# Turning the normalised tokens of two tiles by DMA instead of TensorE, with the instruction order and buffer slots of an adaLN attention and MLP block laid out again

## The chip, the cores and the metric

One core of a Trainium2 chip runs the whole program. The metric is the device time in microseconds of one launch, as the median of several executions. A profile of one execution stands beside it; its span runs from the first to the last instruction.

## The reference

The input is one sequence of 2048 tokens of width 448, in bf16. A conditioning row gives six modulation vectors. The first half of the block normalises the tokens, scales and shifts them, and runs attention with 16 heads of width 28 in which each token looks at itself and at seven earlier tokens, two apart. The second half normalises again, scales, shifts, normalises a third time inside the MLP branch, and applies a two-layer MLP of width 1792.

```python
mod = (silu(c) @ w_mod).reshape(1, 6, 1, 448)
sa, ca, ga, sb, cb, gb = mod[:, 0..5]
h = layernorm(x) * (1 + ca) + sa
x = x + ga * A(h)          # A: qkv, window of 8 with dilation 2, softmax, @ wo
h = layernorm(x) * (1 + cb) + sb
x = x + gb * B(h)          # B: layernorm, gelu(@ w1 + b1), @ w2 + b2
```

## The kernel before

Even and odd tokens are held as two streams (`NS = 2`), so that a dilation of 2 becomes a plain window. There are eight tiles of 2 x 128 tokens and nine attention batches of 2 x 114 queries. Tiles are taken in units: tile 0, tile 1, tiles 2 and 3, tiles 4 and 5, tiles 6 and 7.

For each unit the function `front_ln` issues on VectorE (DVE) the statistics (line 450), their aggregation (452) and the normalisation (470) into a token tile `zy`; the inverse root is made on ScalarE (459 and 461) for tiles 0 and 1, and on GpSimd (466) for the others. A small copy of the last columns, `tail` (480 to 484), completes `zy`. The tokens then have to be turned so that the features stand on the partitions. There are two ways to do it:

- by TensorE: eight transposes for each tile (line 527) into PSUM tiles `ptr`;
- by DMA: one transposing DMA for each tile on SyncE's queue (line 519) into an SBUF tile `zT`.

Either way `affine` (494 on DVE, 496 on ScalarE) scales and shifts the four 128-row pieces into `hT`, from which TensorE makes queries, keys (lines 540, 546, 562) and values (700). For tiles 2 to 7 the queries and keys come out in token order and are turned by DMA too (624).

The other names used below: `c_cols` (line 385) and `mod_cols` (406) are the small matmuls that make the first modulation columns; `sca` (421) adds them up on DVE. `mods` (634) makes the other four modulation rows, `mod_rows` (639) copies them out, and two DMAs (641 and 643) bring them to all partitions as `mod_bc`. `mod_bc` scales the output projection weights on DVE (646), which `out_proj` (797) needs. Then follow the residual (804) and the second and third normalisation, which end in the transposing DMA `yT` (828), and the MLP: first layer at lines 540 and 546, gelu at 858, second layer at 877, final sum at 883, store at 887. `filler` (378) issues products of a tile of zeros; they only keep TensorE occupied.

No scheduler runs on the chip. The code first builds a list of 699 numbered tasks, each with the engines it may run on. The string `ORDER` then lists the numbers in the order of issue. `:A`, `:D`, `:P` put a task on ScalarE, DVE or GpSimd instead of its usual engine, `:R` takes the 64-row part of a sum first, and `55+8@55` puts eight zero products into the PSUM tile of task 55 ahead of it. `SLOTS` gives the memory slot of each buffer in the order in which the buffers are made; a buffer waits until the last reader of its slot is done. Every engine works through its own tasks in that order, SyncE's DMA queue included.

These are the task numbers that matter here:

| tasks | what |
|---|---|
| 17 to 41 | loads on SyncE's queue: 27 is x of tiles 2 and 3, 33 to 36 the four `wmod` pieces for `mods`, 37 to 40 `wo` |
| 55; 63, 64; 68, 69 | `c_cols`; `mod_cols` of the 128-row part; `mod_cols` of the 64-row part |
| 80, 116 | transposes of tiles 0 and 1 by TensorE |
| 95 to 99, 101 to 105 | queries and keys of tile 0 |
| 121 to 126 | queries and keys of tile 1 and their copies |
| 138, 148 | the turn of tile 2 and of tile 3 |
| 149 to 152 | the four `affine` pieces of tiles 2 and 3 |
| 153, 156 | keys and queries of tile 2 |
| 165, 167, 168 | `mods`, its store, `mod_bc` |
| 179, 228 | values of batches 0 and 1 |
| 181, 184; 230, 233 | logits of batch 0; of batch 1 |
| 187, 188 | denominators and outputs of batch 0 |
| 201, 211 | the DMA turn of tiles 4 and 5 |

Of the kernel before, what the change touches and what calls it, by code (L numbers as in the profile page):

```python
# [14 lines left out]
S, D, H, DH, F = 2048, 448, 16, 28, 1792  # L15
# [19 lines left out]
UNITS = [[0], [1], [2, 3], [4, 5], [6, 7]]  # L35
# [5 lines left out]
ENGINE = {"A": "ACT", "D": "DVE", "P": "POOL", "R": "PE2"}  # L41
RATE = 310e3
SLOTS = [
# [6 lines left out]
]  # L50
# [7 lines left out]
232 278 39 40 41 299:R 235 280 211 267 279 268 270 269 300 236 238 281 239 155 158 159 237 304 301 305 271 160:D 302 162  # L58
201 167 215 163 214 212 213 240 225:R 188 226 303 306 282 168 169 170 307 309 191 308 310 311 219:R 220 272 284 241 283
242 245 164 161 312 42 171 313 339 286 285:A 336 221 246 337 340 314 243 216:R 43 44 244 217 290 247 45 46 218 550:A 291  # L60
292 316 317 315 341 318 287:R 288 222 223 248 250 249 338 319 441:P 251 252 320 321 342 127 255 344 322 128 345 334:R
335 369 370 374 323 324 253 254 256 326 257 371 551:R 224 47 48 49 327 325 328 375 372 376 373 552 296 297 343 377 329
331 379 330 332:D 258 260 259 261:A 346 378 380 381 442:R 347 348 50 174 173 351 349 51 289 333 262 382 52 53 443 586:A
352 175 350 353 477:A 405 404 409 408 354 383 355 386 356 387 406 423 426 420:R 421 407 422 410 413 414 411 412 176 357
384 385 388 172 177 358 415:R 418 419 416 436 434 359 361 362 389 391 360 390 392 54 178 363 227 393 396 394 417 364 397
483 395 440 398 484 447 435 448 366 365 444 445 480 481 399 478:R 479 367 400 427 401 402 485 449 446 437 482 486 488
450 452 293 438 294 487 451 453 454 489 490 298 368 403 513 514:R 516 515 518 517 532 535 424 491 492 455 456 457 493
458 495 459 524 526 527 496 494 497 460 461 536 425 498 528 500 499 525 462 463 501 295 502 505 503 504 464 465 466 467
469 519:R 520 521 529 531 522 523 430 431 530 468 470 549 592 553 556 554 557 506 471 558 555 593 594 507 428 472 508
429 432 587 588 474 589 559 560 433 543 544 590 561 591 473 475:A 509 510 511 562 596 595 563 545 546 597 598 476 599  # L70
564 565 566 600 567 568 601 512 623 547 602 548 622 626 627 638:R 639 640 624 625 569 570 628 630 629 633:R 637 632 634
534 636 604 605 603 606 571 573 572 607 609 574 608 610 611 539 575 578 579 614 615 576 612 577 580 540 631 635 537 652
538 653 654 655 581 613 616 617 583 618 619 582 584:A 641 620:A 621 585 644 658 659 661 662 660 533 645 656 541 542 657
663:R 439 667 664 665 666 676 680 677 679 648 646 668 670 669 673:R 674 672 647 649 695 678 675 671 681 683 682 684 696
642 643 650 685 686 651 697 687 688 689 690 698 691 692 693 694
"""


# [73 lines left out]
def kernel(  # L152
# [18 lines left out]
    P = Plan()  # L171
# [302 lines left out]
    def xn(p, n):  # L474
        return x_all[:, p, n * D:(n + 1) * D]
# [26 lines left out]
    def front_ln(u, on_act, dma=False):  # L502
        np_ = len(u)
        if dma:
            zT = sb("yT", [128, NS * KT, 256], BF16, "zT")
        else:
            ptr = [psum("ptr", (128, np_, 2, NS, 128), BF16) for _ in range(2)]
        for q, p in enumerate(u):
            z = fixed("zy", zys)
            for n in range(NS):  # L510
                stats(lambda p=p, n=n: xn(p, n), 0, 2 * p + n, [f"x{p}"])
            rstd(0, 2 * p, 2, on_act)
            for n in range(NS):
                normalize(lambda z=z, n=n: z.t[:, n, 0:D], lambda p=p, n=n: xn(p, n), 0, 2 * p + n, [f"x{p}"],
                          bufs=[z], writes=[(z, n)])
            tail(z, [(z, 0), (z, 1)], (z, 2), p == 0)
            zk = [(z, 0), (z, 1), (z, 2)]
            if dma:
                add("SP", 2.0, lambda z=z, q=q: nc.sync.dma_start_transpose(
                    out=zT.t[:, :, 128 * q:128 * q + 128], in_=z.t[:].rearrange("p n e -> p (n e)")), reads=zk, bufs=[z, zT],  # L520
                    writes=[(zT, q)], xfer=1.0, name=f"zT{p}")
                continue

            def tr(q=q, z=z):
                for kt in range(KT):
                    for n in range(NS):
                        nc.tensor.transpose(out=ptr[kt % 2].t[:, q, kt // 2, n, :], in_=z.t[:, n, kt * 128:(kt + 1) * 128], identity=ident[:])
# [373 lines left out]
    for pi, (batches, tiles) in enumerate(PHASES):  # L901
        exps.clear()
        lt_mms.clear()
        for i in batches:
            if i < 3:
                front_ln(UNITS[i + 2], False, dma=i > 0)
                if UNITS[i + 2][0] in NATURAL:
                    for p in UNITS[i + 2]:
                        natural_qk(p)
                else:  # L910
                    front_qk(UNITS[i + 2])
            if i == 0:
                mods()
            attention(i, tbl, prev_w1)
            while done < NP and (128 * (done + 1) - 1) // SBQ <= i:
                out_proj(done)
                done += 1
        tg = add("ACT", 1.28, lambda: nc.scalar.preload_act_table_set(GELU_SET), after=list(exps), name="tbl")
        gelus.clear()
        w1_mms.clear()  # L920
        for t in tiles:
            mlp(t, tg, list(lt_mms))
        prev_w1 = list(w1_mms)
        if pi < len(PHASES) - 1:
            tbl = add("ACT", 1.28, lambda: nc.scalar.preload_act_table_set(EXP_SET), after=list(gelus), name="tbl")
# [30 lines left out]
```

## Time and profile before

| what | us |
|---|---|
| median of 3 executions | 173.84 (173.5 to 174.85) |
| the profiled execution | 173.98 |
| its span | 171.9 |
| TensorE busy | 163.9 |
| DVE busy | 116.0 |
| ScalarE busy | 107.6 |
| GpSimd busy | 46.2 |

The profiled execution is 2.1 us longer than its span and 0.14 us above the median. In the lists of the trace each row starts with the start and the length in us, then engine, line and operation, output and inputs, shape and count; in square brackets stands how long the engine had been idle, and who ended that. "PE" is TensorE's multiplication, "PEld" its weight load; a name ending in q is an engine's sequencer, so that "SPq" is SyncE issuing DMAs. A matmul's length is longer than its share of the engine, because matmuls overlap: twelve that start one after the other 0.19 us apart are each shown as 0.35 us long. What one costs is the distance between starts.

### The profile page before, as it was taken

The page shows a single profiled execution, that of the slowest core. Times are in us where ns is not written, and L with a number is a line of the kernel's source. Part 1 is how long each engine was busy: PE and PEld are TensorE (multiplying, and loading weights), DVE is VectorE, ACT ScalarE, POOL GpSimd, SP SyncE. Part 2 cuts the span into 40 slices and gives each one's busy share as a digit, 9 for nine tenths or more (in the row PEclk, how much of TensorE's full clock was granted, in tenths as well). Part 3 has the DMA queues.
Part 4 walks back from the last instruction along what each step waited for, and adds up shares of the span by engine and source line. Part 5 has one row for each costly group of instructions (what it writes and reads, how often), then busy time and mean ns, then how long its engine had stood idle before and what let it go on. Part 6 is the DMA issues. An engine that isn't in the chain of part 4 may idle for free.

```text
span 171.9 us, 5019 instructions
## 1 busy us (share of the span) xinstructions
PE 163.9 (95%) x2142; PEld 84.5 (49%) x2142; DVE 116.0 (67%) x282; ACT 107.6 (63%) x149; POOL 46.2 (27%) x76
## 2 busy tenths in 40 slices
PE   5699998999999999999999999999999999999992
PEld 3476654455545543345454345555334543445562
DVE  5648989698999989998644895756997704001032
ACT  3437999989489993789896569664285402817000
POOL 3270611600260401525005701130113701930000
PEclk9999999999999999999999999999999999999999
DMA  5999908799999999102540000151100063100013
GB/s 160 342 300 400 206 6 96 153 197 160 232 240 210 227 165 251 21 0 53 75 65 6 0 0 4 57 106 20 53 0 0 0 122 125 39 0 0 0 57 107
DMA packets 33462, 18.27 MB, mean 106 GB/s; under 512 B 26395, under 2 KB 32480, under 8 KB 33440
## 3 DMA queue, kind: packets, MB, share of 16 engines
q1 hardware_dynamic: 33436, 17.95, 45.8%
q8 instruction: 17, 0.28, 0.7%
q14 instruction: 5, 0.04, 0.1%
q10 hardware_dynamic: 4, 0.00, 0.0%
HBM read 9.81 MB, written 1.84 MB: 68 GB/s over the span
## 4 chain that ended last, share of the span: by engine, by line
PE 61%; DVE 21%; DMA 6%; ACT 4%; POOL 3%; issue 2%; SPq 0%; POOLq 0%; DVEq 0%
PE p L877 23%; PE p L540 22%; DVE stt L450 8%; PE pw L797 5%; PE p L546 4%; DVE zy L470 3%; DMA yT<-zy 2%; POOL rs_all L466 2%; PE ps_col L378 2%; DMA mod_bc<-mod_hbm 2%; DVE mvs L452 2%; DVE h L813 2%; DVE et L745 2%; DMA x_all<-in_A_x_dram 2%; ACT hm L858 1%
## 5 line engine op out<-in xcount | busy, mean ns | idle before, releaser
L858 ACT ACTIVATE hm<-p,b_col 128x512 bf16<-128x512 f32 x56 | 33.9, 689 | 30.7 <-PE p L546 26.2
L877 PE MATMUL p<-w_s,hm 128*128 128x448 bf16 (+1 forms) x238 | 44.1, 342 | 0.0
L540 PE MATMUL p<-yT,w_s 128*128 128x512 bf16 x168 | 38.5, 380 | 0.6 <-DMA yT<-zy 0.6
L466 POOL TENSOR_TENSOR rs_all<-tv_all,neg_half 128x2 f32<-128x2 f32 x22 | 16.7, 764 | 59.3 <-DVE tv_all L464 51.8
L877 PEld LDWEIGHTS <-hm 128*128 128x128 bf16 x238 | 22.8, 98 | 19.2 <-issue 0.4
L883 DVE TENSOR_TENSOR x_all<-p,x1p 128x896 bf16<-128x896 f32 (+2 forms) x10 | 8.8, 900 | 27.6 <-PE p L877 27.6
L540 PEld LDWEIGHTS <-w_s 128*128 128x128 bf16 x168 | 15.6, 98 | 22.2 <-issue 4.4
L450 DVE BATCH_NORM_STATS2 stt<-x_all 128x6 f32<-128x448 bf16 x32 | 19.0, 611 | 0.6 <-DMA x_all<-in_A_x_dram 0.5
L739 ACT ACTIVATE et<-lt 128x928 bf16<-128x928 f32 x18 | 16.1, 948 | 2.4 <-PE lt L732 2.3
L835 POOL TENSOR_TENSOR x1p<-x_all,gbb_bc 128x448 f32<-128x448 bf16 x16 | 16.3, 1047 | 0.2 <-issue 0.2
L540 PE MATMUL pq<-wqk_st,hT 128*128 128x448 bf16 x72 | 15.2, 354 | 0.0
L782 DVE TENSOR_TENSOR qT<-po,den 128x912 bf16<-128x912 f32 x9 | 9.8, 1104 | 6.0 <-ACT den L776 6.0
L745 DVE TENSOR_TENSOR et<-et,mask 128x928 bf16<-128x928 bf16 x18 | 11.1, 641 | 3.4 <-ACT et L739 3.2
L797 PE MATMUL pw<-wo_s,qT 128*128 128x448 bf16 x64 | 12.8, 353 | 0.1
L621 ACT CAST zy<-pq 128x896 bf16<-128x896 f32 x11 | 10.0, 910 | 1.7 <-PE pq L546 0.9
L804 DVE TENSOR_TENSOR x_all<-pw,x_all 128x896 bf16<-128x896 f32 x8 | 8.7, 1086 | 3.4 <-PE pw L797 3.3
L813 DVE TENSOR_TENSOR h<-h,mod_bc 128x896 bf16<-128x896 bf16 x16 | 10.6, 665 | 0.2
L540 PEld LDWEIGHTS <-hT 128*128 128x128 bf16 x72 | 6.4, 98 | 7.0 <-issue 1.8
L776 ACT ACTIVATE den<-den,den_bias 128x928 f32<-128x928 f32 x9 | 9.5, 1066 | 0.2
L774 ACT ACTIVATE den<-pd 128x928 f32<-128x928 f32 x9 | 8.4, 948 | 1.8 <-DVE qT L782 1.2
L450 DVE BATCH_NORM_STATS2 stt<-h 128x6 f32<-128x448 bf16 x16 | 9.3, 613 | 0.2
L470 DVE TENSOR_SCALAR zy<-h,mvs,rs_all 128x448 bf16<-128x448 bf16 x16 | 8.6, 579 | 1.1 <-POOL rs_all L466 1.0
(113 smaller groups left out, 190.9 us busy)
## 6 DMA issues: line engine op xcount, KB each, us to landing
w_s<-in_B_w_dram SPq DMA_DIRECT2D x7, 224.0 KB
out_dram<-x_all SPq DMA_DIRECT2D x7, 224.0 KB, 2.1
x_all<-in_A_x_dram SPq DMA_DIRECT2D x3, 448.0 KB, 6.2
wmod<-in_w_mod_dram SPq DMA_DIRECT2D x3, 448.0 KB, 8.7
w_s<-in_B_w_dram SPq DMA_DIRECT2D x3, 448.0 KB
wqk_st<-in_A_wqkv_dram SPq DMA_DIRECT2D x3, 225.0 KB
wm_st<-in_w_mod_dram SPq DMA_DIRECT2D x1, 672.0 KB, 4.6
x_all<-in_A_x_dram SPq DMA_DIRECT2D x2, 224.0 KB
```

The source lines that it names most:

```text
L450: add("DVE", 0.53, lambda: nc.vector.bn_stats(out=stt[:, w, b, :], in_=src()), reads=reads, bufs=bufs, after=early if w == b == 0 else (), ...
L466: add("POOL", 0.55 + 0.17 * n, lambda: nc.gpsimd.tensor_tensor(out=r, in0=tv, in1=neg_half[:, 0:n], op=ALU.pow), reads=[f"tv{w}_{b0}", "ne ...
L470: add("DVE", 0.31, lambda: nc.vector.tensor_scalar(out=dst(), in0=src(), scalar1=mvs[:, w, b, 0:1], scalar2=rs_all[:, w, b:b + 1], op0=ALU ...
L540: nc.tensor.matmul(out(), lhsT=lhs(kt, slice(0, 128)), rhs=rhs(kt, slice(0, 128)), start=first and kt == 0, stop=not first and kt == KT - 2)
L621: add("ACT", 0.80, lambda to=to, src=src: nc.scalar.copy(out=to(), in_=src()), bufs=[pq, st], reads=["zpad"], writes=[(st, 0)], name="evac ...
L739: exps.append(add("ACT", 0.83, lambda half=half, lt=lt: nc.scalar.activation(out=et.t[:, 2 * half:2 * half + 2].rearrange("p r m c -> p r ...
L745: nc.vector.tensor_tensor(out=ev, in0=ev, in1=mask[:], op=ALU.mult)
L797: nc.tensor.matmul(pw.t[:, s, 0:D], lhsT=qT[:, KT * s + ft, LEAD + 128 * p:LEAD + 128 * p + 128], rhs=wo_s[:, ft, :], start=(ft == 0), sto ...
L813: add("DVE", 0.55, lambda vec=vec, op=op: nc.vector.tensor_tensor(out=h2.t[:], in0=h2.t[:], in1=vec.unsqueeze(1).to_broadcast([128, NS, D] ...
L835: add("POOL", 1.0, lambda n=n: nc.gpsimd.tensor_tensor(out=x1p.t[:, n, :], in0=xn(p, n), in1=gbb2_bc[:], op=ALU.add), reads=[f"x{p}", "gbb ...
L858: gelus.append(add("ACT", 0.585, lambda f=f, a=a, p1=p1s[g]: nc.scalar.activation(out=hm.t[:, f].rearrange("p n c -> p (n c)"), in_=p1.t[: ...
L877: nc.tensor.matmul(p2.t[:, n, 0:c1 - c0], lhsT=hm.t[:, f, n, q * 128:(q + 1) * 128], rhs=w2_s[:, f, c0:c1], start=(f == parts[0][0]), stop ...
```

## The change

`front_ln` is now called with `dma=True` for the unit of tiles 2 and 3 as well. Its two PSUM tiles `ptr` give way to one SBUF tile `zT`, so there is one buffer less. Tasks 138 and 148 move from TensorE to SyncE's queue, and the numbers of all other tasks stay. `SLOTS` and `ORDER` are written anew as a whole; their beginnings are shown here.

```diff
 SLOTS = [
-    0, 1, 1, 1, 0, 0, 1, 1, 2, 0, 3, 0, 1, 2, 0, 3, 1, 0, 2, 1, 3, 1, 2, 3, ...
+    1, 0, 1, 0, 0, 1, 3, 1, 0, 2, 3, 0, 1, 0, 2, 3, 2, 2, 3, 0, 1, 3, 2, 1, ...
 ORDER = """
-17 18 0 15 14 1 55+8@55 9 12 5 3 10 2 13 19 20 21 22 91:P 23 24 25 26 92:P 87:P 93:P 94:P 88:P 89:P 7 27 28 16 56 73 74
-11 6 71 57 58 72 75 59 60 76 78 77 67 61 79 63+14@63 66 62 85:A 90:A 68+3@68 69 64 4 65 70 80 81 29 30 83 95+5@95 101 82
-102 103 109 107 108 110 86:A 111 31 96 97 84 104 32 33 34 35 105 112 98 114 113 115:A 106 116 139 120:A 118:A 117:A
-119:A 131 36 37 99 100 132 129 130 133 134 179 180 121 122:R 123 141 140 142 143 144 136 135 137 146 145 273 204 205 38
-138 8 147 148 151 152:A 150:A 202 203 206 124 125:R 126 184 185 181 182 149 156:R 157 153 207 208 192 193 209 210:D 275
-183 194 186 195 154 196 276 274 277 197 230 233 231 165 166 187 234 228+5@228 189 190 229 265 266 263 264 199 198 200
+17 15 14 16 0 1 2 9 13 6 11 12 18 5 73 74 71 72 3 10 19 20 21 22 86:P 91:P 23 24 55+11@55 56 57 58 59 75 60 85:P 76 77
+68+12@68 67 66 69 78 79 63+4@63 61 62 64 4 65 25 70 26 89:P 90:A 27 80 92:A 83 81 101+13@101 93:A 82 107 102 103 109
+95+2@95 108 110 84 111 112 113 114 28 94:P 104 105:R 115:A 116 106 96 87:P 7 120:A 97 118:A 29 141 30 31 32 88:P 98 99:R
+33 139 142 129 100 140 143 144 131 179 184 181 130 132 133 134 145 146 147:D 148 135 136 192 137 119:A 117:A 121:R 122
+182 124:R 125 138 194 8 193 204 195 196 185 186 183 197 187 123 180 188 199 198 126:D 230 149:A 189 200 233 231 234 151
+150 152 153+3@153 154 34 35 156:R 157 263 264 275 205 202 203 206 265 207 209 232 235 208 201 190 191 266 267 210:D 273
 ...
-                front_ln(UNITS[i + 2], False, dma=i > 0)
+                front_ln(UNITS[i + 2], False, dma=True)
```

The zero products of the order before are 8 at task 55, 14 at 63, 3 at 68, 5 at 95 and 5 at 228, 35 in all. In the order after they are 11 at task 55, 12 at 68, 4 at 63, 13 at 101, 2 at 95, 3 at 153 and 5 at 228, 50 in all. The seventh to ninth entries of `SLOTS` are the PSUM slots of `c_cols` and of the two `mod_cols`: 1, 1, 2 before and 3, 1, 0 after. On SyncE's queue the order after is: load 33, turn of tile 3, turn of tile 2, loads 34 and 35, turn of tile 4, loads 36 and 37, then the turned keys and queries of tile 2, the turn of tile 5, the store of `mods`, loads 38 to 40, and `mod_bc`. Before, loads 33 to 41 were issued first, then the turns.

More of the change, by code (lines that the diff above doesn't have):

```diff
@@ L61 @@
[L61 to L75, printed above, removed]
+17 15 14 16 0 1 2 9 13 6 11 12 18 5 73 74 71 72 3 10 19 20 21 22 86:P 91:P 23 24 55+11@55 56 57 58 59 75 60 85:P 76 77
@@ new lines @@
+228+5@228 229 36 165 37 268 155 158 269 274 276 270 277 211 166 236 299:R 238 167 278 280 239 279 281 212 271 214 215
+159:R 301 300 160 304 237 240 38 213:A 39 162:R 302 303 225 305 40 163 306 307 168 169 170 272 308 309 310 311 226 282
+219:R 220 286 241 441:A 285:A 242 243 245 312 313 161 164 216 336 339 284:A 316 283:A 550:P 290:R 337 314 315 317 318
+244 41 221 42 43 44 45 227 340 341 217 319 218 321 287 46 291 288 320 322 338 222:R 223 246 247 248 323 326 342 250 127
+128 249 324 251 252 344 345 253 255 327 256 325 328 329 369:R 370 289 47 334 335 371 372 373 374 254 257 375 296 297 376
@@ new lines @@
+551:R 552 224 48 378 49 377 258 330 331 332:D 259 379 260 333 343 346 380 381 261 262 50 442:R 443 347 348 382 349 351
+352 383 386 384 405 404 408 420:R 409 421 422 410 406 407 415:R 51 171 477:P 350 353 385 387 388 52 53 177 176 54 292
+389 354 391 390 173 355 356 175 413 412 414 411 172 436 392 393 419 357 416 417 418 394 395 396 178 397 398 399 423 434
+174 358 400 427 359 360 361 362 363 364 426 401 402:D 403 440 480 444 481 445 483 435 293 447 484 294 478:R 446 365 366
+367:A 485 482 486 437 448 488 449 450 479:D 487 451 438 452 489 453 454 368 514:R 513 515 516 518 517 455 532 536 534
@@ new lines @@
+535 490 491 524 528 526 586:A 525 527 492 456 459 457 519:R 520 523 533 529:R 460 521 495 425 493 496 458 461 424 462
+430 431 463 464 494 465 295 298 592 531 530 522 549 593 556 553 554 497 498 428 429 587 499 500 466 469 501 557 502 470
+505 506 467 468 471 503 555 558 560 559 432 588 589 504 594 472 474 473 590 507 508 509 475:D 510 561 511:D 591 543 544
+596 595 545 546 562 563 564 439 433 597 598 599 565 568 566 600 601 547 569 567 570 604 602 512 476 623 622 624 625
+638:R 639 626 640 641 627 571 573 572 605 603 606 607 608 609 574 628 631 630 632 633:R 629 610 611 575 578 576 577 612
@@ L76 @@
+614 637 579 615 580 613 616 581 582 654 537 538 539 617 583 619 618 620 584 635 585 644 621 652 634 636 645 653 655 540
+658 660 662 659 661 548 656 541 676 678 642 663:R 667 664 666 648 665 657 542 649 668 672 671 677 673:R 681 670 669 674
+675 683 684 695 682 646 647 696 687 685 643 680 697 679 698 686 650 651 688 689 690 691 692 693 694
 """
```

3 lines of the change are left out of this document (removed), and 12 rows, old and new, of the table SLOTS.

## The prediction

> **What bounds the kernel now.** The first views read are the busy lines of the page with its table of slices, then the busy time by stage, then the chain of work that ended last.
>
> ```profile
> PE 163.9 (95%) x2142; PEld 84.5 (49%) x2142; DVE 116.0 (67%) x282; ACT 107.6 (63%) x149; POOL 46.2 (27%) x76
> ...
> PEclk9999999999999999999999999999999999999999
> DMA  5999908799999999102540000151100063100013
> ```
>
> ```profile
> 11.87:41.42 29.55, 28.74 (x614) 16.51 (x613) 25.82 (x68) 26.19 (x36) 8.04 (x15) 1.00 0.87 185
> 41.42:64.72 23.30, 22.67 (x394) 11.62 (x395) 22.21 (x50) 20.27 (x24) 6.01 (x6) 1.00 0.99 206
> 64.72:169.00 104.28, 103.97 (x1062) 50.48 (x1062) 61.68 (x129) 57.30 (x83) 26.77 (x35) 1.00 0.20 45
> ```
>
> ```profile
> 5.81 3.15 PE ps_col L378 x14
> ...
> 10.58 0.76 PE ptr L527 x8
> ...
> 13.78 0.70 DVE zy L470 x2
> 14.48 1.07 DVE stt L450 x2
> ...
> 60.55 4.03 DMA yT<-zy
> 64.58 0.14 issue
> 64.72 2.75 PE p L540 x12
> ```
>
> In a stage row the first number behind the stage is its length, the next is TensorE's busy time, then come its weight loads, DVE, ScalarE and GpSimd. From 64.72 us, where the MLP begins, TensorE is busy 103.97 of 104.28 us. From 11.87, where the first sums start, to 41.42 it is busy 28.74 of 29.55, and to 64.72 another 22.67 of 23.30. So TensorE bounds everything from 11.87 on. The chain names DVE and a DMA ahead of 64.72, but TensorE waits there for 0.6 us only: both would have to come sooner to bring a gain. A change pays by starting TensorE sooner, by taking work from it, or by taking away one of its few waits, and costs what new waits it brings.
>
> **The start.** These are the rows of TensorE and of who waits for it.
>
> ```profile
> 1.26 1.89 PE L378 MATMUL ps_c<-warm_w 128*128 128x256 bf16 x8 [1.26 <-DVE warm_w L242]
> ...
> 3.42 0.60 PE L385 MATMUL ps_c<-one,c_row 1*128 1x128 bf16 x4 [0.28 <-DMA c_row<-in_c_dram]
> ...
> 5.81 3.15 PE L378 MATMUL ps_col<-warm_w 128*128 128x256 bf16 x14 [1.79 <-DVE silu_bf L392]
> ...
> 10.62 0.17 DVE L421 TENSOR_TENSOR mod_col<-ps_col,add_col 128x8 f32<-128x8 f32 x1 [2.98 <-PE ps_col L406]
> ...
> 11.16 0.71 PE L378 MATMUL pq<-warm_w 128*128 128x256 bf16 x5
> 11.25 1.02 ACT L496 ACTIVATE hT<-ptr,mod_col 128x256 bf16<-128x256 bf16 x2 [3.36 <-PE ptr L527]
> ...
> 11.87 1.58 PE L562 MATMUL pq<-hT,Wqk 128*128 128x256 bf16 x12
> ```
>
> The fourteen zero products at 5.81 waited 1.79 us for `silu_bf`, because their PSUM tile has the slot of `c_cols` (both 1), which `silu` reads. DVE then stood still for 2.98 us and ScalarE for 3.36. Starts lie about 0.21 us apart in the first two groups (3.15 less a last length of 0.4, over 13) and about 0.11 in the third (0.71 less 0.27, over 4).
>
> In the new slots the three tiles have slots 3, 1 and 0, so the twelve products of task 68 need not wait for `silu`. Eleven products from 1.26 end at 1.26 + 11 x 0.21 = 3.6, `c_cols` at 4.2, and twelve more at 6.7. The `mod_cols` take about 1 us (from 8.96, where the row of 5.81 ends, to 10.58, less 0.6 for three zero products between), and four products 0.4 to 0.8. The transposes of tile 0 then run from about 8.4 to 9.1 instead of 10.58 to 11.34: some 2 us sooner for DVE and ScalarE. But thirteen zero products now stand ahead of the first sums instead of five. At 0.11 they take 1.4 us, and the first sums start at about 10.5 to 10.8, as ScalarE, which makes its second piece of `hT` 1.02 us after the transposes, also allows. I take 10.8, a gain of 1.1. One bound is 10.3, a gain of 1.6. The other is thirteen at 0.21, which is 2.7 us: 11.8 to 12.1, a loss of up to 0.2.
>
> **The turns of tiles 2 and 3.** These rows bear on what is taken from TensorE and on what the DMA costs.
>
> ```profile
> 19.51 1.08 PE L527 MATMUL ptr<-ident,zy 128*128 128x128 bf16 x16
> 20.43 0.82 PE L540 MATMUL pq<-hT,Wqk 128*128 128x256 bf16 x6
> ...
> 22.27 0.70 PE L732 MATMUL lt<-qT,kT 28*64 28x58 bf16 x64
> 23.06 0.37 PE L546 MATMUL pq<-wqr_st,hT 64*128 64x448 bf16 x2
> ...
> 27.37 0.54 PE L754 MATMUL pd<-et,ones_k 64*32 64x464 bf16 x8
> ...
> 32.49 0.87 PEld L540 LDWEIGHTS <-hT 128*128 128x128 bf16 x6 [0.21 <-issue]
> ...
> 34.03 0.68 PE L765 MATMUL po<-et,vb 64*32 64x57 bf16 x64
> ```
>
> ```profile
> L335 SPq DMA_DIRECT2D x_all<-in_A_x_dram x5: 397/468/586, 0.8 to 9.4; - x5
> ...
> DMA to landing us min/median/max: 6.2/6.2/6.2
> ```
>
> ```profile
> L358 SPq DMA_DIRECT2D wmod<-in_w_mod_dram x4: 328/480/665, 10.0 to 13.7; - x4
> ...
> DMA to landing us min/median/max: 8.5/8.6/8.9
> ```
>
> ```profile
> L494 DVE TENSOR_SCALAR hT<-zT,mod_col x7: 403/406/501, 35.1 to 45.8; 128x512 bf16<-128x512 bf16 x7
> L519 SPq DMA_TRANSPOSE zT<-zy x4: 1232/1286/2126, 25.1 to 35.4; - x4
> ...
> DMA to landing us min/median/max: 3.2/3.2/3.2
> ```
>
> Taken away: from 19.51 to the next start at 20.43 the sixteen transposes hold TensorE for 0.92 us. That is the second term.
>
> Added: two issues of 1.3 us on SyncE, 3.2 us each from issue to landing. When are they issued? The x of tiles 2 and 3 is asked for at 6.4 and lands 6.2 us later, at 12.6. DVE then has four statistics (two in 1.07), two normalisations (0.70 both) and about 1 us of small pieces, some 4 us in all: tile 3 is ready near 16.6, and the second turn is issued at 17.9. The last load ahead of them, the first `wmod` piece, is asked for at 10.0 and lands at 18.6 by its row. Undisturbed the two land at 19.8 and 21.1. Were they as slow as the loads, 8.6 us each, they would land at 25.2 and 26.5. I take 21.5, nearer the first, because the other three `wmod` pieces are now issued behind them, and because the DMA row of the page shows 0 tenths in its slice from 21.5: the loads are done by then.
>
> When does TensorE need them? Before, it began the queries of tile 2 at 23.06. It does the same work now except 0.92 for transposes, starts 1.1 sooner, and has the denominators and outputs of batch 0 and the logits of batch 1 ahead of them (0.54, 0.68 and 0.70 by the rows of 27.37, 34.03 and 22.27). So 23.06 - 0.92 - 1.1 + 1.9 is 22.9. `hT` comes after the landing and after DVE has copied the keys of tile 1 (task 126, moved from ScalarE; 1024 columns, when line 804 below takes 1.10 for 896: 1.25 us, from about 21 to 22.2), plus three DVE pieces of 0.41: 23.4. Three zero products fill this hole, and TensorE loses about 0.5. Bounds: nothing, or 26.5 + 1.2 - 22.9 = 4.8.
>
> DVE gets this copy (1.25) and gives back a smaller one (task 160, 1.1) and three pieces of `hT` to ScalarE; nothing there is on TensorE's path while DVE is 1 to 2 us ahead. What would stand behind a late copy 126 is the `hT` of tile 2.
>
> **The modulation rows.**
>
> ```profile
> 28.52 0.71 PE L378 MATMUL pv<-warm_w 128*128 128x256 bf16 x5 [0.61 <-ACT mod_rows L639]
> ...
> 32.48 0.56 SPq L641 DMA_DIRECT2D mod_hbm<-mod_rows  x1
> ...
> 34.73 0.54 SPq L643 DMA_DIRECT2D mod_bc<-mod_hbm  x1
> ```
>
> ```profile
> 34.73 3.35 DMA mod_bc<-mod_hbm
> ...
> 41.42 1.70 PE pw L797 x8
> 43.15 1.10 DVE x_all L804
> ```
>
> `mods` and the values of batch 1 had one PSUM slot (3), so TensorE waited 0.61 us for `mod_rows`. Now the values come first and `mods` has slot 0, and this wait is gone: 0.61.
>
> SyncE now waits for tile 3, tile 2 and tile 4 ahead of the last `wmod` piece. Tile 4 should be ready near 21.8, the load is issued near 23.2, and `mods` is reached at 22.9 + 0.5 + 3.0 (two sums, as from 32.49 to 34.03) + 2.0 (a sum and five zero products) = 28.4. With a landing of 3.2 the load is there at 26.4, with 8.6 at 31.8. So it is hidden by 2 us, or costs 3.4. I take nothing, for the loads it would have to stand behind are gone by then. `mod_rows` then ends near 30, the store goes out behind the turn of tile 5 near 31.4, three `wo` loads follow, and `mod_bc` leaves near 33.7 and lands 3.35 later, at 37 to 38.3. TensorE wants the output projection at 41.42 - 2.1 = 39.3. The cover is 1 us; each us later than that costs one.
>
> **The MLP's start and what follows.** `yT` must come sooner by as much as TensorE does. Its chain on DVE starts with the residual at 43.15, which follows the output projection, so it moves with TensorE; its pieces are the same, less one piece of `hT`. Behind 64.72 the same work stands in nearly the same order and TensorE has 0.31 us of idle time: no change.
>
> The sum: - 1.1 (start) - 0.92 (transposes) - 0.61 (wait for `mod_rows`) + 0.5 (wait for `hT`) = - 2.1 us. Against the profiled execution of 173.98 that is 171.9; the median lies 0.14 lower, so the forecast is 171.7 us. A measurement of this kernel tells about 1% from no change, which is 1.74 us here; the forecast is just outside.
>
> **The rivals.** First: the two turns stand in line behind the loads and land as late as these, at 26.5. TensorE, which works in order, then idles 4.8 us instead of 0.5 at the queries of tile 2: 171.7 + 4.3 = 176.0, slower. It decides from a landing 2.1 us later than I take (23.6) on, where the gain is spent. For it speaks the 8.6 us of `wmod`; against it, that the last load ahead has landed by 18.6. [...]
>
> Second: the change has more zero products, 50 for 35, not fewer as its words say, and the thirteen run at the slow pace. The first sums start at 12.1 and the term is + 0.2 in place of - 1.1: 173.0. For it speaks the 0.21 in the first two groups; against it, that TensorE would have been busy without a gap since 1.26. The granted clock shows nothing of this, it is 9 in every slice. The Trainium skill (TensorE: Matmul & The Clock Gate, Part 1) says that the array runs at half its clock until it has been busy for a window of about 3.4 us; by that rule the thirteen run at 0.11, and the pair of 0.21 and 0.11 agrees.
>
> Third: SyncE's waits push the last `wmod` piece or `mod_bc` past their cover. The price is up to 3.4 us, on the way about 2: 174.
>
> Fourth: DVE does not get ahead, `yT` lands at 64.6 as before, and TensorE waits at the MLP for what it gained: 173.8. For it speaks DVE's 22.21 of 23.30 us in that stage.
>
> **How the numbers follow.** The forecast has 0.55, with its own range of 170.2 (start at 10.3, no wait for `hT`, 1.0 less, and 0.5 for shifts behind 64.72) to 172.7 (1.0 of small new waits); 0.05 of it lies within 1%. The first rival has 0.16, slower; the second 0.11, within 1%; the third 0.11, of which 0.04 slower; the fourth 0.07, within 1%. That gives faster 0.50, same 0.30, slower 0.20. The range for 8 in 10 goes from 170.2 to 176.0, the first rival's time, beyond which lie a late `hT` and a late `mod_bc` together.
>
> **What would show it.** Right: the DVE's `sca` near 8.8 instead of 10.62, the first sums (line 562) near 10.8, no transposes after tile 1, `zT` landing by 21.5, line 797 starting near 39.3 and the MLP near 62.6. Wrong: a hole in TensorE of over 1 us ahead of the queries of tile 2 or of `mods`, an idle DVE ahead of line 646 with TensorE waiting behind it, or the MLP starting at 64.7 or later although line 797 came sooner.

## The result and the profile after

The changed kernel took **175.98 us** (median of four executions, 175.76 to 177.57) against 173.84 for the kernel before: a ratio of 1.0152 [1.0114, 1.019], slower. Run again in twelve executions against 29 of the kernel before (median 173.94), its median was 175.48 (173.62 to 178.4) and the ratio 1.0063 [1.0033, 1.0094]. It is slower in both, by 1.5% and by 0.6%. (A ratio leaves out executions over 1.5% above the fastest of their kernel, so it can differ from that of the medians.) Its times scatter more; one reason for that is found below. The profiled execution took 175.76 us, 1.78 more than that of before; its span is 2.2 us longer.

First the clock's row of the page's table of slices, then the three stages by time, cut at the first sums, at the first output projection and at the start of the MLP. Behind a stage stand its length, TensorE's busy time, weight loads, DVE, ScalarE, GpSimd, and the granted clock.

```profile
PEclk9999978999999999999999999999999999999999
```

```profile
10.24:41.20 30.96, 29.49 (x604) 16.41 (x602) 23.78 (x67) 24.35 (x32) 9.05 (x20) 0.94 0.88 191
41.20:66.59 25.39, 23.05 (x395) 11.63 (x395) 21.34 (x47) 21.33 (x25) 6.84 (x8) 1.00 1.06 195
66.59:171.00 104.41, 104.03 (x1062) 50.82 (x1062) 61.45 (x134) 56.69 (x80) 25.82 (x34) 1.00 0.22 49
```

The first sums start 1.63 us sooner than before. By the output projection 1.41 of that is gone, because the stage takes 30.96 us instead of 29.55; by the MLP the kernel is 1.87 us behind, because the second stage takes 25.39 instead of 23.30. From there to the end of the span little changes (0.3 us). The clock row has a dip that was not there before, and the first stage's mean clock is 0.94.

The start and the turns, from the timeline of after:

```profile
8.39 0.17 DVE L421 TENSOR_TENSOR mod_col<-ps_col,add_col 128x8 f32<-128x8 f32 x1 [0.79 <-PE ps_col L406]
...
8.81 1.59 PE L378 MATMUL pq<-warm_w 128*128 128x256 bf16 x13
10.24 0.82 PE L562 MATMUL pq<-hT,Wqk 128*128 128x256 bf16 x6
...
15.78 2.81 SPq L519 DMA_TRANSPOSE zT<-zy  x2
...
21.70 1.06 DVE L494 TENSOR_SCALAR hT<-zT,mod_col 128x512 bf16<-128x512 bf16 x3
```

DVE's `sca` is at 8.39 instead of 10.62, the thirteen zero products take 0.11 us each, and the turns of tiles 2 and 3 have landed by 21.70. All this is about as predicted. Then comes the hole (two rests of TensorE close to each other); TensorE's and ScalarE's timelines:

```profile
20.51 0.69 PE L765 MATMUL po<-et,vb 64*32 64x57 bf16 x64
21.83 0.70 PE L732 MATMUL lt<-qT,kT 28*64 28x58 bf16 x64 [0.63 <-DVE kT L603]
23.38 0.49 PE L378 MATMUL pq<-warm_w 128*128 128x256 bf16 x3 [0.85 <-ACT den L774]
23.71 1.98 PE L540 MATMUL pq<-wqk_st,hT 128*128 128x448 bf16 x6
```

```profile
21.69 0.81 ACT L496 ACTIVATE hT<-zT,mod_col 128x512 bf16<-128x512 bf16 x1 [1.23 <-DMA zT<-zy]
22.41 0.92 ACT L774 ACTIVATE den<-pd 128x928 f32<-128x928 f32 x1
```

Two rests of TensorE: 0.63 us for DVE's copy of the keys of tile 1 (task 126), which the logits of batch 1 read, and 0.85 for a PSUM slot. The three zero products and the keys of tile 2 have the slot of the denominators of batch 0, and ScalarE reads these only at 22.41: the task that reads them (189) stands behind its piece of `hT` (149), which waits 1.23 us for the turn. What follows is seen in the two windows behind, by the granted clock (the last figure but two of a row):

```profile
21.00:24.00 3.00, 1.53 (x94) 1.27 (x82) 2.96 (x8) 2.31 (x3) 0.00 (x1) 1.00 0.99 323
24.00:28.00 4.00, 4.00 (x16) 1.21 (x14) 3.30 (x10) 1.90 (x3) 0.69 (x1) 0.57 1.11 128
```

In 24 to 28 us TensorE runs at a mean clock of 0.57 and starts 16 matmuls; a group of six takes 1.98 us, where the same group takes 1.30 at full clock (in `no_hole`, below). At 0.57 the four microseconds lose 4 x 0.43 = 1.7. Later in the same timeline, with SyncE and DVE:

```profile
31.79 1.23 SPq L519 DMA_TRANSPOSE zT<-zy  x1
...
35.16 1.11 SPq L643 DMA_DIRECT2D mod_bc<-mod_hbm  x1
...
40.52 1.16 DVE L646 TENSOR_TENSOR wo_s<-wo_s,mod_bc 128x896 bf16<-128x896 bf16 x2 [1.81 <-DMA mod_bc<-mod_hbm]
...
47.61 0.36 PE L546 MATMUL pq<-wqr_st,hT 64*128 64x448 bf16 x2 [0.88 <-DVE x_all L804]
...
51.09 3.70 SPq L624 DMA_TRANSPOSE kT<-zy  x1
...
56.81 0.70 PE L732 MATMUL lt<-qT,kT 28*64 28x58 bf16 x64 [1.29 <-DMA kT<-zy]
...
66.59 1.67 PE L540 MATMUL p<-yT,w_s 128*128 128x512 bf16 x7 [0.17 <-DMA yT<-zy]
```

The second stage has two new rests: 0.88 us for a residual on DVE, and 1.29 for the keys of tile 4, whose turn goes out at 51.09 and takes 3.70 us to issue, where the turn of 31.79 takes 1.23. Together they are 2.17 us, and the stage is 2.09 longer. For `yT` TensorE waits 0.17 us, less than the 0.63 of before.

### The profile page after: what moved, and what is told of

Read it like the earlier page. It is cut to its first block, busy times and chain, and to the rows that moved or that the text cites. A ratio compares the mean times of both kernels' runs of the same rounds, so it can differ in the third digit from the quotient of the medians.

```text
span 174.1 us, 5025 instructions
## 1 busy us (share of the span) xinstructions
PE 165.5 (95%) x2141; PEld 85.2 (49%) x2141; DVE 114.0 (66%) x285; ACT 107.1 (62%) x146; POOL 45.2 (26%) x76
## 4 chain that ended last, share of the span: by engine, by line
PE 51%; DVE 11%; DMA 9%; issue 2%; ACT 2%; SPq 2%; POOL 1%; POOLq 0%; DVEq 0%
PE p L877 22%; PE p L540 16%; DMA zT<-zy 4%; PE pw L797 3%; DMA kT<-zy 3%; PE p L546 3%; DMA w_s<-in_B_w_dram 2%; DVE zy L470 2%; ACT et L739 2%; DVE w_s L654 2%; DVE stt L450 2%; PE pq L540 2%; PE po L765 1%; DVE x_all L804 1%; SPq L828 1%
## 5 line engine op out<-in xcount | busy, mean ns | idle before, releaser
L877 PEld LDWEIGHTS <-hm 128*128 128x128 bf16 x238 | 22.8, 98 | 19.2 <-issue 0.4
L540 PEld LDWEIGHTS <-w_s 128*128 128x128 bf16 x168 | 15.6, 98 | 21.4 <-issue 4.1
L540 PE MATMUL pq<-wqk_st,hT 128*128 128x448 bf16 x72 | 16.5, 374 | 0.0
L745 DVE TENSOR_TENSOR et<-et,mask 128x928 bf16<-128x928 bf16 x18 | 11.9, 674 | 2.3 <-ACT et L739 2.0
L621 ACT CAST zy<-pq 128x896 bf16<-128x896 f32 x12 | 10.6, 907 | 3.9 <-PE pq L540 1.5
L813 DVE TENSOR_TENSOR h<-h,mod_bc 128x896 bf16<-128x896 bf16 x16 | 9.7, 620 | 0.2
L797 PEld LDWEIGHTS <-qT 128*128 128x128 bf16 x64 | 6.2, 98 | 6.2 <-DVE qT L782 0.3
```

Source lines behind the costliest of these rows:

```text
L540: nc.tensor.matmul(out(), lhsT=lhs(kt, slice(0, 128)), rhs=rhs(kt, slice(0, 128)), start=first and kt == 0, stop=not first and kt == KT - 2)
L621: add("ACT", 0.80, lambda to=to, src=src: nc.scalar.copy(out=to(), in_=src()), bufs=[pq, st], reads=["zpad"], writes=[(st, 0)], name="evac ...
L745: nc.vector.tensor_tensor(out=ev, in0=ev, in1=mask[:], op=ALU.mult)
L797: nc.tensor.matmul(pw.t[:, s, 0:D], lhsT=qT[:, KT * s + ft, LEAD + 128 * p:LEAD + 128 * p + 128], rhs=wo_s[:, ft, :], start=(ft == 0), sto ...
L877: nc.tensor.matmul(p2.t[:, n, 0:c1 - c0], lhsT=hm.t[:, f, n, q * 128:(q + 1) * 128], rhs=w2_s[:, f, c0:c1], start=(f == parts[0][0]), stop ...
```

## The experiments

Edits are given in the task numbers of `ORDER`. Medians of the kernel before in these sessions were between 173.79 and 174.03.

**The two halves of the change.** `dma_only` is the kernel before with its own order and slots and the turns of tiles 2 and 3 by DMA.

```diff
-                front_ln(UNITS[i + 2], False, dma=i > 0)
+                front_ln(UNITS[i + 2], False, dma=True)
```

> The order and slots of before, with only the turns of tiles 2 and 3 by DMA; both turns stand behind two of the four wo loads on SyncE's queue. First theory (a hole in TensorE ahead of the queries of tile 2 makes the clock gate close, and this is what costs): tile 2 is ready at 19 and tile 3 at 20.3, the turns land near 24 to 25, hT near 26, so TensorE stands still from 22.0 to 26 and the next 3.4 us run at half clock: 175 to 177 us. Second theory (the loads that the new order puts behind the turns are what costs): here no load of note is behind them, so only the hole of about 4 us less the 0.9 us of transposes shows in the stage, part of it is made up later, and the time is 174 to 176 us, with a full clock.

`start_only` is the kernel before with the start of the changed one, and TensorE still turns tiles 2 and 3.

```diff
 ORDER: as in the changed kernel up to task 81, then as before, with
-95+5@95
+95+13@95
 SLOTS of the three PSUM tiles at the start:
-1, 1, 2
+3, 1, 2
```

> The kernel before with only the start of the new order: its constants, mod_cols, zero products and PSUM slots up to the first sums; tiles 2 and 3 are turned by TensorE. If TensorE bounds everything from the first sums on, as the prediction held, these start near 10.3 instead of 11.87 and the time falls by 1.1 to 1.6 us, to 172.3 to 172.8. If the stage up to the MLP is bound by what does not start sooner (the landing of x of the later tiles, mod_bc, the chain on DVE), the MLP starts at 64.7 as before and the time stays at 173.5 to 174.

`dma_only` took 180.46 us, ratio 1.0365 [1.0308, 1.0421]; `start_only` 172.61, ratio 0.9931 [0.9897, 0.9966]. Timelines of `dma_only` (SyncE, TensorE), then two pieces of the chain of `start_only`:

```profile
9.97 3.81 SPq L358 DMA_DIRECT2D wmod<-in_w_mod_dram  x4
13.82 1.01 SPq L362 DMA_DIRECT2D wo_s<-in_A_wo_dram  x2
18.62 3.28 SPq L519 DMA_TRANSPOSE zT<-zy  x2
...
26.37 0.56 PE L546 MATMUL pq<-wqr_st,hT 64*128 64x448 bf16 x2 [4.49 <-ACT hT L496]
27.26 4.38 PE L540 MATMUL pq<-wqk_st,hT 128*128 128x448 bf16 x12 [0.33 <-DVE hT L494]
```

```profile
40.37 3.20 PE pw L797 x16
...
63.33 1.89 PE p L540 x8
```

In the old order the turns cost TensorE 4.49 us at one stroke, after which twelve matmuls take 4.38 us where six take 1.30 at full clock: more than either theory gave. The mean clock of all four executions is 0.98. The six loads ahead of the turns are only part of the cause. The turns are issued 2.84 us later than in the changed kernel (18.62 for 15.78), because DVE normalises the two tiles at 17.41 and 18.39 instead of 14.79 and 15.79. From the first issue to the first piece of `hT` it then takes 6.9 us instead of 5.9 (25.51 and 21.69, on ScalarE). So of the 3.8 us by which `hT` starts later, about 1 can be the loads' and 2.8 are the later tiles'. The new order has the tiles ready sooner and sends three of the four `wmod` pieces behind the turns; no run does one without the other. The start alone is worth 1.2 us (1.18 by the medians), its whole predicted 1.1, and it reaches the MLP at 63.33, 1.39 sooner than before. `start_only` beats both kernels and remained the fastest of all.

**The hole.** `no_hole` lets ScalarE free the slot first and puts six zero products in front of the logits of batch 1.

```diff
-149:A
...
-189
+189 149:A
...
-230
+230+6@230
```

> The changed kernel with two edits: the logarithm of the denominators of batch 0 stands ahead of the ScalarE piece of hT, so that its PSUM slot is free about 0.8 us sooner, and six zero products stand ahead of the logits of batch 1. First theory (clock): TensorE no longer rests near 21 and 22.5, the granted clock stays 1.00 between 24 and 28, the queries of tile 2 end 1.7 us sooner, and the time falls by about 1.7 us to 174.3. Second theory (line of DMAs): the clock is whole but mod_bc, the hT of tiles 6 and 7 and the keys of tile 4 land nearly as late as they did, and the time stays within 0.6 us, 175.4 to 176.

It took 173.81 us, ratio 0.996 [0.9927, 0.9993]; the medians of all executions, 173.81 and 173.79, show no difference from the kernel before. Its windows and timeline:

```profile
21.00:24.00 3.00, 3.00 (x150) 2.30 (x148) 3.00 (x7) 2.72 (x5) 0.29 (x1) 1.00 1.01 300
24.00:28.00 4.00, 4.00 (x30) 1.97 (x30) 3.62 (x11) 3.15 (x5) 0.69 (x1) 1.00 1.09 182
```

```profile
21.27 0.69 PE L765 MATMUL po<-et,vb 64*32 64x57 bf16 x64
...
23.62 1.30 PE L540 MATMUL pq<-wqk_st,hT 128*128 128x448 bf16 x6
...
39.49 3.21 PE L797 MATMUL pw<-wo_s,qT 128*128 128x448 bf16 x16
...
45.73 0.36 PE L546 MATMUL pq<-wqr_st,hT 64*128 64x448 bf16 x2 [0.94 <-DVE x_all L804]
...
54.55 0.70 PE L732 MATMUL lt<-qT,kT 28*64 28x58 bf16 x64 [0.91 <-DMA kT<-zy]
...
64.03 2.32 PE L540 MATMUL p<-yT,w_s 128*128 128x512 bf16 x10
```

TensorE is busy throughout, the clock stays at 1.00, and the output projection starts at 39.49. Both prices of the hole are gained. This execution began its first sums later than that of after, at 10.99 instead of 10.24, and the outputs of batch 0 come 0.76 later too (21.27 for 20.51). Yet the keys of tile 2 start at 23.62 instead of 23.71, so 0.85 us of rest are gone; from there to the output projection it takes 15.87 us instead of 17.49, which is 1.6 of clock. The two edits were then tried one by one, `swap_only` (189 ahead of 149) and `fill_only` (the six products, ahead of the logits of batch 1 as in `no_hole`).

> The changed kernel with one edit of no_hole alone: ScalarE takes the reciprocal of the denominators of batch 0 (task 189) ahead of its piece of hT (task 149), so that the PSUM slot comes free before TensorE's three zero products and the queries need it; the six zero products ahead of the keys of tile 2 are not added. The theory that the sum of two rests lets the clock fall: the rest of 0.85 us goes or shrinks below 0.4, 0.63 us at line 732 stays, no slice of 24 to 28 us has a granted clock below 0.9, line 797 starts near 39.7 and the median is 174.0 to 174.4, as no_hole's 173.81. The theory that the added zero products are what kept the clock up in no_hole: the half clock stays (about 0.6 in 24 to 28), line 797 starts at 40.8 or later, and the median is 175.0 to 175.5, only the rest itself gained.

> The changed kernel with the other edit of no_hole alone: six zero products ahead of task 230, ScalarE's order as in the changed kernel, so that the rest of 0.85 us behind its piece of hT stays. The theory that the sum of two rests lets the clock fall: both rests stay (0.6 and 0.8), the clock is 0.6 in 24 to 28 us in the profile or in about half of the runs, the median is 175.3 to 176.0. The theory that the added zero products are what kept the clock up: clock above 0.9 in 24 to 28 us, line 797 near 40.0, median 174.2 to 174.6.

`swap_only` took 174.19 us, ratio 0.9968 [0.9926, 1.001]; `fill_only` 174.54, ratio 1.0017 [0.9982, 1.0052]. Windows and TensorE's timeline of `swap_only`:

```profile
21.00:24.00 3.00, 2.39 (x136) 1.81 (x116) 2.90 (x7) 2.81 (x4) 0.29 (x1) 1.00 1.05 290
24.00:28.00 4.00, 4.00 (x34) 1.81 (x31) 3.65 (x10) 3.34 (x4) 0.69 (x1) 1.00 1.35 225
```

```profile
22.14 0.70 PE L732 MATMUL lt<-qT,kT 28*64 28x58 bf16 x64 [0.61 <-DVE kT L603]
```

The same of `fill_only`, with two later windows:

```profile
23.34 0.49 PE L378 MATMUL pq<-warm_w 128*128 128x256 bf16 x3 [0.61 <-ACT den L774]
```

```profile
24.00:28.00 4.00, 4.00 (x31) 1.94 (x30) 3.31 (x10) 3.14 (x5) 0.69 (x1) 1.00 0.66 145
52.00:56.00 4.00, 2.50 (x83) 1.42 (x80) 3.31 (x10) 3.04 (x4) 0.50 (x1) 1.00 0.94 186
56.00:60.00 4.00, 4.00 (x153) 2.25 (x151) 2.87 (x9) 3.48 (x5) 1.84 (x4) 1.00 1.00 160
```

Each edit leaves one rest of 0.61 us and takes away the other, and with either the clock stays up here. `swap_only` came out as the first theory said, with an output projection sooner still (38.99 for 39.7). For `fill_only` this theory expected both rests to stay, and that was wrong: the six products fill the time of the copy of the keys, so that its result (clock up, 174.54) is the one that the second theory gave. The added products are not needed to keep the clock up, since `swap_only` has none. Both kernels have one rest where after has two, and a clock below 0.995 is listed for two of twelve executions of `swap_only` and one of twelve of `fill_only`. That makes the sum of the rests, 1.48 within 3 us, the likely cause.

**The kernel unchanged, again.**

> The changed kernel itself, beside the variants that it is compared with: 175.5 to 176.5 us, with the half clock of about 3.4 us after the rests of TensorE near 21 and 22.5.

The twelve executions fall into two halves by the granted clock that is listed with each. Six at about 1.0 have a median of 174.51 (173.62 to 175.34), six at 0.981 to 0.99 one of 176.21 (175.61 to 178.4). The difference is 1.7 us, the price worked out above, though two of the slower six, at 0.981, lost about twice as much clock as the others. The profile is of one of the slower six, and shows the same hole and the same fall:

```profile
21.00:24.00 3.00, 1.44 (x137) 1.29 (x130) 2.96 (x7) 1.72 (x3) 0.29 (x1) 0.97 1.01 290
24.00:28.00 4.00, 4.00 (x16) 1.52 (x16) 3.65 (x11) 2.10 (x3) 0.69 (x1) 0.60 0.95 193
```

In the first four executions the halves do not separate: 175.8 and 176.16 us at a clock of 1.0, 175.76 and 177.57 at 0.99. So the clock falls in eight of sixteen executions; where it falls in those without a profile is not known. Even without a fall the changed kernel is no faster than the one before (174.51 against 173.94).

**The modulation loads.** `wo_early` puts the three late `wo` loads (38 to 40) ahead of the first turn of keys (155), so that they do not stand between `mod_rows` and `mod_bc`.

> The changed kernel with the three late wo loads issued before the turned keys of tile 2 instead of between the store of mods and mod_bc; SyncE is idle there from 23.8 to 27.2. Second theory (line of DMAs): mod_bc is issued 1.3 us sooner and lands up to 2 us sooner, the turns of tiles 6 and 7 too, the MLP starts 1 to 2 us sooner, time 174 to 175. First theory (clock): the half clock between 24 and 28 stays and with it the late omul and the late turn of tile 5 on which mod_bc waits; the time stays at 175.5 to 176.

It took 174.6 us, ratio 0.9997 [0.9961, 1.0033], and again split: six executions at full clock had a median of 174.01, six below 176.31. `mod_bc` was issued at 33.53 instead of 35.16 and DVE no longer waited for it, but TensorE waited 1.0 us for the last `wmod` piece, and the MLP began at 66.34, only 0.25 sooner. The median is in the range of the second theory. In its profile the clock fell elsewhere:

```profile
21.00:24.00 3.00, 1.41 (x82) 1.16 (x70) 2.97 (x7) 2.30 (x3) 0.20 (x1) 1.00 0.95 269
...
52.00:56.00 4.00, 2.50 (x85) 1.44 (x82) 3.52 (x10) 3.00 (x5) 0.29 (x1) 1.00 0.78 167
56.00:60.00 4.00, 4.00 (x15) 1.22 (x15) 2.88 (x9) 2.46 (x3) 1.69 (x3) 0.57 1.00 141
```

The same 2.50 us of work in 52 to 56 was followed by 1.00 in `fill_only` (above) and by 0.57 here. And in the same execution of `wo_early` 1.41 us of work in 21 to 24 was followed by a clock of 1.00 (its row of 24 to 28 says so). So the amount of rest alone does not decide in a single execution.

The clock's own records in the traces show what else does. After the record of full clock at the start (7.11 us in after, 6.73 in `after_again`, 5.10 in `wo_early`, 10.75 in `dma_only`) the clock falls to one half 17.07, 17.07, 51.20 and 13.65 us later, which is 5, 5, 15 and 4 steps of 3.41, and it stays there for one step (two in `dma_only`). Counted in such steps, the hole of the two profiles of after lies in a single one, in which TensorE is busy 1.95 of 3.42 us (20.76 to 24.18) and 2.02 of 3.41. In `wo_early` the same hole is divided between two steps, with 2.46 and 2.75 us of work, and nothing falls. Where the steps begin differs from execution to execution, which would explain that the same hole costs clock in only some of them. Work in a step is not the whole rule either: 1.91 us were followed by half clock in `wo_early` (52.89 to 56.30), 1.92 by full clock in `fill_only` (51.54 to 54.96).

**Where the rest of the gain stays.** `no_hole` starts the output projection 0.88 us sooner than `start_only` and the MLP 0.70 later. The edits below are made to `no_hole`. `hT_later` moves a piece of `hT` that waits for its turn (286) behind a residual (313) on DVE; `w1_later` moves three loads of the first layer's weights (43 to 45) behind the turn of the keys of tile 4 (218); `both_later` does both.

```diff
 hT_later:          -286   ...   -313          +313 286
 w1_later:          -43 44 45   ...   -218     +218 43 44 45
 w1_behind_keys:    -43 44 45   ...   -289     +289 43 44 45
 w2_behind_y:       w1_behind_keys, and -48 -49   ...   -262   +262 48 49
```

> The kernel without the two rests (no_hole) with one more edit: the DVE piece of hT of tiles 6 and 7 stands behind the second residual instead of ahead of the first. There DVE waited 1.23 us for the turn of tile 7 with the residuals queued behind it, and TensorE 0.94 us for the second residual's PSUM slot. If that is one of the two places where the gain went, this rest goes, DVE's chain to the MLP starts 1.2 us sooner, and the time falls by 0.9 us against no_hole, to 172.3 to 173. If the late keys of tile 4 bind alone, the rest ahead of the logits of batch 4 grows from 0.9 to 1.8 us and the time stays with no_hole, 173 to 173.8.

> The kernel without the two rests (no_hole) with one more edit: the three large loads of w1 are issued behind the turned keys of tile 4 instead of ahead of them and of the turned queries of tile 5. If the turns stand in line behind these loads, the keys of tile 4 land 2 to 3 us sooner, TensorE's rest of 0.9 us ahead of the logits of batch 4 goes, and the time falls by 0.9 us, to 172.3 to 173. If DVE's late residuals bind the MLP's start, or if the later loads delay w2 and its scaling, the time stays at 173 to 173.8 or rises.

> Both edits on the kernel without the two rests. If the three places (the rests with the clock, the waiting piece of hT, the keys of tile 4 behind w1) hold the whole of what the prediction missed, TensorE runs without a rest over 0.3 us from 23 to the MLP, the MLP starts near 62.3 and the time is 171.4 to 172.2, which is the sum of the prediction. If something else binds the MLP's start (yT, w2), the MLP starts at 63.5 or later and the time is 172.6 to 173.6.

`hT_later` took 175.76 us in only six executions (172.19 to 176.67), too scattered to tell; in its profile the rest for the residual is gone and the one for the keys of tile 4 has grown to 2.01. `w1_later` took 173.6, ratio 0.9968 [0.9946, 0.999], `both_later` 173.58, ratio 0.9971 [0.9946, 0.9997]. In both the rest for the keys is gone and another has come. `w1_later`, DVE and TensorE:

```profile
57.91 0.70 DVE L470 TENSOR_SCALAR zy<-h,mvs,rs_all 128x448 bf16<-128x448 bf16 x2 [1.00 <-DMA kT<-zy]
```

```profile
63.70 1.67 PE L540 MATMUL p<-yT,w_s 128*128 128x512 bf16 x7 [0.71 <-DMA yT<-zy]
```

The normalised tokens that `yT` turns go into a buffer from which the keys of tile 6 had not been turned yet, behind the loads. So these loads went behind that turn as well (`w1_behind_keys`), and then two loads of the second layer's weights (48, 49) behind the turns of `yT` (`w2_behind_y`).

> no_hole with the three loads of the first layer's weights (tasks 43, 44, 45) moved further back than in w1_later: behind the turn of the keys of tile 6 (task 289). In w1_later DVE stood still for 1.00 us at 57.9 because the normalised tokens for yT go into a buffer that this turn of keys had not yet read; TensorE waited 0.71 us for yT at 63.70. The theory that the loads ahead of that turn make it land late: DVE's rest at line 470 falls below 0.3, both turns of yT leave about 0.8 us sooner, the MLP starts at 62.8 to 63.2 and the median is 172.6 to 173.1. The theory that the transfers are bound by the DMA engines as a whole, so that a later load only moves the wait: yT or the weights themselves land late, the MLP starts at 63.6 or later, the median is 173.4 to 174.0.

> w1_behind_keys with the two loads of the second layer's weights that stand ahead of the turns of yT (tasks 48, 49) moved behind these turns (behind task 262). In w1_behind_keys DVE had the normalised tokens ready without a rest, but the two turns took 5.10 us to issue behind the loads of 50.55, 52.13 and 54.57, and TensorE waited 2.10 us for yT at 64.24. The theory that the turns of yT are held up by the transfers in flight when they are issued: they issue in about 3.5 us, the MLP starts at 62.3 to 63.0, the median is 172.3 to 173.2. The theory that what holds them up are the three loads of the first layer's weights alone, or that the second layer's weights come too late: the MLP starts at 63.6 or later, or TensorE waits over 0.5 us at line 877 near 70, and the median is 173.6 to 174.6.

They took 174.55 us, ratio 1.0 [0.9961, 1.0039], and 173.96, ratio 0.9985 [0.9948, 1.0021]. SyncE and TensorE of the first, then of the second with its waits from 65 us on:

```profile
56.88 5.10 SPq L828 DMA_TRANSPOSE yT<-zy  x2
...
58.95 3.19 PE L797 MATMUL pw<-wo_s,qT 128*128 128x448 bf16 x16
64.24 2.76 PE L540 MATMUL p<-yT,w_s 128*128 128x512 bf16 x12 [2.10 <-DMA yT<-zy]
```

```profile
57.61 3.76 SPq L828 DMA_TRANSPOSE yT<-zy  x2
...
63.70 2.75 PE L540 MATMUL p<-yT,w_s 128*128 128x512 bf16 x12 [0.80 <-DVE stt L450]
```

```profile
PE pd L754 <- DVE et L745: 1.6, 1, 1.6
```

DVE's rest at line 470 is gone, as the first theory said, but the two turns of `yT` then take 5.10 us to issue behind the loads, and TensorE, which is 1.94 us ahead of before at the second output projection (58.95 for 60.89), waits 2.10 for them. With two more loads out of the way they issue in 3.76, TensorE still waits 0.80, and a new wait of 1.6 us comes behind the start of the MLP. Each move of a load took one wait away and brought another elsewhere. The MLP of `w1_behind_keys` starts as late as its second theory said, with a median (174.55) above that theory's range; that the DMA engines as a whole are the limit, which it gave as the reason, is not shown.

## Why the prediction was wrong

The direction was wrong: 171.7 us was forecast, faster, and 175.98 measured. That this is the first rival's 176.0 is chance: its late landing did not happen, and the time was lost in other places. By its steps:

- **The start, - 1.1: right.** The first sums came at 10.24, a little before the 10.3 of the better bound, and the start alone brought 1.18 us (first sums at 10.40 in that profile). The thirteen zero products ran at 0.11; the second rival is out.
- **The transposes and `mod_rows`, - 0.92 and - 0.61: right together.** TensorE no longer waits for `mod_rows`, and with the hole closed the output projection starts at 39.49, where 39.3 was worked out. From the first sums to there `no_hole` takes 28.50 us and `start_only`, which has neither term, 29.97: 1.47 less, near the 1.53 of the two. They were not measured one by one.
- **The landing of the turns at 21.5: right** (a piece of `hT` starts at 21.70), by another way: the two are issued from 15.78 to 18.59, sooner than the 16.6 to 19.2 worked out, and take longer to land than the 3.2 us of the rows. The first rival did not happen. A wait of its size came in `dma_only`, 4.49 us, for the greater part because the tiles were ready later. The Trainium skill (DMA: Bandwidth & Descriptors, "Queues, rings and completion order") has an engine take a queue's descriptors in ring order; `dma_only` agrees as far as it goes: the last of the four `wmod` loads ahead, issued at 13.3, landed 8.1 us later at 21.4, and `hT` could start at 25.5.
- **The wait for `hT`, + 0.5: this is the first step that failed.** It cost 0.63 + 0.85 = 1.48 us of rest and 1.7 us of clock. The prediction worked out that copy 126 would end near 22.2 and asked what stands behind it on DVE; it did not ask what TensorE reads from it, which is the logits of batch 1. And it let "three zero products fill this hole", without asking whose PSUM slot they write: they waited for that slot themselves.
- **The clock** was read as 9 in every slice and taken as a constant. That a rest could lower it was in no term and no rival. (The row says 9 at the start too, where the zero products lie 0.21 us apart: the trace of before has its first record of the clock at 11.08 us, full, and there the spacing falls to 0.11.) From 10.24 to the output projection the account is: 0.56 better at the start, 0.98 more rest, 1.7 of clock, in sum 2.1 later than the 39.3 forecast, which is 41.4; 41.20 was measured.
- **`mod_bc`, cover of 1 us: too short.** It left at 35.16 and DVE could use it at 40.52, 5.4 us later where 3.35 was taken and later than the 37 to 38.3 worked out. That cost TensorE's weights only 0.3 us, because TensorE was late too.
- **The second stage, put at nothing: the second step that failed.** From the output projection to the MLP the kernel before took 23.30 us, after took 25.39, and `no_hole` 24.54. `yT` did move with TensorE in after, which waited only 0.17 us for it. The prediction looked at that last wait alone. It had no term for new waits on the way, and two came: 0.88 us for a residual, which is queued on DVE behind a piece of `hT` that waits for its turn (it is gone in `hT_later`, where that piece is moved, but also in `w1_later`, where only loads are, so its cause stays open), and 1.29 us for the keys of tile 4, whose turn stands behind three loads (it is gone in all four kernels with these loads moved). Its range had 1.0 us for small new waits. With the loads moved, TensorE does wait for `yT`, 2.10 us in `w1_behind_keys`: the fourth rival's place, though DVE's load, the cause named there, does not stand ahead of its two turns, which take 5.10 us to issue. The keys, the weights and `yT` share SyncE's queue. What of the 1.24 us that `no_hole` is longer than before comes from more turns in flight, and what from the new order of all tasks, was not separated.

The two failed steps make up the miss: about 1.9 us at 41.20 and 2.1 more by 66.59, against 3.86 between the forecast and the time of the profiled execution.

## What to carry to other kernels

When work leaves TensorE, follow every tile that TensorE reads next to its last writer, and every PSUM slot to its last reader, the zero products' own slots included: a filler that shares a slot with what is late fills nothing. Give rests of TensorE that lie close together two prices, their length and the half clock that may follow, and time a kernel that has them in many executions. And before sending a product through a DMA queue, look whether later turns in that queue are already just in time; here the start alone was worth 1.2 us, and with the turns on top, hole closed, less was left than without them (173.81 us in `no_hole`, 172.61 in `start_only`; the rest of the order differs too).

## What the runs showed of the hardware

Two rests of TensorE of 0.63 and 0.85 us, 1.53 us of work in 3, were enough for a mean clock of 0.57 over the next 4 us, which is 3.4 us at half; no rest reached 1 us. The falls of four profiles lie 4, 5, 5 and 15 steps of 3.41 us behind the first record of full clock, and last one or two steps.

How often a clock below 0.995 is listed, by kernel:

| kernel | executions with a fall |
|---|---|
| before | 1 of 114 |
| `start_only` | 0 of 11 |
| changed kernel | 8 of 16 |
| `wo_early`, both rests | 6 of 12 |
| `swap_only`, `fill_only`, one rest | 2 and 1 of 12 |
| `no_hole`, neither | 1 of 12 |
| `hT_later`, on `no_hole` | 3 of 6 |
| `w1_later`, `both_later`, `w1_behind_keys`, `w2_behind_y`, on `no_hole` | 0, 1, 4 and 2 of 12 |
| `dma_only` | 4 of 4 |

The five kernels made from `no_hole` have other rests later. The clock is not all of the scatter: `no_hole` ranges from 172.35 to 175.48 us without a fall.

The Trainium skill (TensorE: Matmul & The Clock Gate, Part 1) gives the default half rate after an idle window of about 3.4 us and calls that window free-running. The length of the dip, its steps and its coming and going from run to run agree with that; the window before the dip was not idle here, but busy 1.95 of 3.42 us.

The turn by DMA takes SyncE 1.23 us to issue when little is in flight, as at 31.79 in after, and 3.70 at 51.09, behind three loads and the turn of some queries.
